# Attention and a sinkhorn-routed expert layer: raw first-layer weights on another queue and in another group, sums behind the adds in group 0, quarter products turned round in the fast pairs

## The chip, the cores and the metric

The kernel runs on one core of a Trainium2 chip. The time is device microseconds (us) of one execution. The engines of the core work side by side, each through its own instructions in order: TensorE (PE in the profile; PEld is its weight load), VectorE (DVE), ScalarE (ACT), GpSimd (POOL) and SyncE (SP). SP, ACT and POOL also issue DMAs. An engine that meets an instruction whose semaphore is not yet up stands still, and everything behind it on that engine stands with it.

## The reference

Inputs: local queries, keys and values of 8 batches x 8 heads x 512 x 64, and 32 global ones for each batch and head. Two steps:

```python
# attention: global rows see all; local row i sees the globals and local j with |i - j| <= 32
out_g = sm(scale * q_g @ k_all.T) @ v_all
out_l = sm(concat(scale * q_l @ k_g.T, masked(scale * q_l @ k_l.T))) @ concat(v_g, v_l)
x = rows of concat(out_g, out_l)             # 4352 tokens x 512
# expert layer: P is a 4352 x 8 matrix, normalised by rows and columns 8 times
P = sinkhorn(exp(x @ w_gate - max))
out = sum over e of P[:, e] * (relu(x @ w1[e]) @ w2[e])     # w1[e]: 512 x 1024, w2[e]: 1024 x 512
```

## The kernel before

Tokens are cut into nine groups: m = 0 to 7 of 512 local tokens, m = 8 with the 256 global ones. The first stage (to about 396 us) does the attention, the routing matrix and, in the gaps, the first layers of experts 0 to 3, whose hidden values go to DRAM (`hd`). The second stage, which the change touches, walks over *units* (m, e), with e in the order 4, 0, 5, 1, 6, 2, 7, 3. Unit i stands for m = i // 8. Units come in *pairs* of an even unit i (expert 4, 5, 6 or 7, whose first layer is still to be computed) and an odd unit i + 1 (expert 0 to 3, hidden values loaded by `load_h`). Pair 8 is units 8 and 9, the first of group 1; group 0 holds pairs 0, 2, 4, 6.

**The second layer** is a seven-product scheme: `product(i, q)`, q = 1 to 7, is 8 matmuls of 256 columns (2 token blocks x 4); q = 5, 2 and 1 take the sums `s` that `sums(i)` made on DVE, q = 6 and 7 the differences that `sums` wrote back into h, and q = 3 and 4 take h as it is. Products 1 to 5 add up in five fixed PSUM banks over the whole group; products 6 and 7 of a pair share two of three rotating banks (r0, r1, r2) and `add` (line 945, DVE) puts them into the output tile o in the odd unit. In the last unit of a group (`closes`) all banks are added to o, and `store` writes o out.

**The first layer of unit i + 2** is woven into the even body i: in the plain form `l1`, eight matmul groups of 4 x 512 columns, the first three of them before product 3; they use the same three rotating banks, so the second group needs the bank of product 6 and the third that of product 7 of the odd unit before.

**The fast form** (`class Fast`) takes two halves p = 0, 1 of 28 matmuls of 256 columns each, half 0 in body i - 2, half 1 in body i - 1, with stages s0 to s3: s0 (products 1 and 5 into banks H and Q, copied by ACT), s1 (2 and 6, and a DVE add X at line 862), s2 (7 and 3, and a DVE add Y at line 869), s3 (4 onto H). H sits in bank r0, whose last reader is the relu of s3 of the half before. It needs sums of first-layer weights. `WX` says from which group on an expert is fast. `prep_w1` makes the sums: a *raw piece* (half of an expert's w1, four strided DMAs of 128 KB, line 727) is loaded into a weight buffer, four DVE subtractions or additions (line 689) complete it, and POOL stores it to DRAM (`w1c`, line 742), from where it is loaded as a whole later (line 730). I call the four raw pieces R60, R61 (expert 6) and R70, R71 (expert 7).

**Queues.** `wseq` is the written order of all weight loads, plain ones (line 721, 1 MB), raw pieces and `w1c`. `load_w1` runs through it on SP, two ahead of use; all of them share the two buffers of the tag `w1e`. On SP they stand in one line with `load_pb` (row factors, line 753, 256 KB, two for a pair), `load_x` (line 770, once a group) and `load_h` (line 805, 1 MB). The order of all instructions is written by hand (`manual_schedule`). In an even plain body the DVE order is `sums(i + 1)`, `scale_x(i + 4)`, weight sums of the second layer in group 0 (`prep_w2c`, five instructions), `scale_h(i + 3)`, `prep_w1`; in an odd body `sums(i + 1)`, then the adds of products 6 and 7.

Of the kernel before, what the change touches and what calls it, by code (L numbers as in the profile page):

```python
# [23 lines left out]
def kernel(  # L24
# [13 lines left out]
    nc = tc.nc  # L38
# [3 lines left out]
    D, E = moe_w_gate.shape  # L42
# [30 lines left out]
    NL = E // 2  # L73
# [1 line left out]
    xd = [ydram.tile([P, DP, n], FP16, name=f"xd{m}") for m, (_, n) in enumerate(groups)]  # L75
    w1d = [ydram.tile([P, DP, F], FP16, name=f"w1d{e}") for e in range(NL, E)]
    pd = ydram.tile([E, NTOK], FP32, name="pd")
    WX = {6: 1, 7: 2}
    w1c = {e: [ydram.tile([P, 7, 2, 256], FP16, name=f"w1c{e}_{p}") for p in range(2)] for e in WX}
    psx = ExitStack()  # L80
    xpool = psx.enter_context(tc.tile_pool(name="xpool", bufs=1, side="right"))
# [623 lines left out]
    def fast(i):  # L705
        return i < NUN and units[i][0] < B and units[i][0] >= WX.get(units[i][1], B)

    wseq = [(i, p) for i in range(0, NUN, 2) for p in ((0, 1) if fast(i) else (None,))]
    for e, m in WX.items():
        for p in range(2):  # L710
            wseq.insert(wseq.index((E * m + 2 * p, None)), (e, "raw", p))
    raw = {}
    wnext = 0

    def load_w1(used):
        nonlocal wnext
        while wnext < len(wseq) and (wnext < 2 or wseq[wnext - 2] in used):
            i, *p = wseq[wnext]
            if p[0] is None:
                w = w1s[i] = wpool.tile([P, DP, F], FP16, tag="w1e", name="w1s")  # L720
                nc.sync.dma_start(out=w, in_=w1d[units[i][1] - NL])
            else:
                w = wpool.tile([P, 7, 2, 256], FP16, tag="w1e", name="w1q")
                if p[0] == "raw":
                    for o, r, k in ((0, 0, 0), (1, 0, 1), (3, 1, 0), (2, 1, 1)):
                        f0 = 512 * r + 256 * p[1]
                        nc.sync.dma_start(out=w[:, o], in_=w1d[i - NL][:, 2 * k : 2 * k + 2, f0 : f0 + 256])
                    raw[wseq[wnext]] = w
                else:
                    nc.sync.dma_start(out=w, in_=w1c[units[i][1]][p[0]])  # L730
                    w1s[(i, p[0])] = w
            wnext += 1
            if wnext < 2:
                return

    def prep_w1():
        for k in list(raw):
            w = raw.pop(k)
            for o, a, b, op in ((5, 0, 3, ALU.subtract), (3, 3, 2, ALU.add), (4, 3, 0, ALU.subtract),
                                (6, 1, 4, ALU.subtract)):  # L740
                tt(w[:, o], w[:, a], w[:, b], op)
            nc.gpsimd.dma_start(out=w1c[k[0]][k[2]], in_=w)
            used.add(k)
# [136 lines left out]
    def sums(i, k0=0, k1=HF, part=(0, 1)):  # L880
        if i >= NUN - 1:
            return
        n = groups[units[i][0]][1]
        t1, t2 = slice(0, n // 2), slice(n // 2, n)
        h = hs[i]
        if i not in ss:
            new_s(i)
        s = ss[i][:, :, k0:k1]
        lo, hi = h[:, k0:k1], h[:, HF + k0 : HF + k1]
        if 0 in part:  # L890
            tt(s[:, 0:2, :, 0 : n // 2], lo[:, :, 0:n].rearrange("p k (a t) -> p a k t", a=2),
               hi[:, :, 0:n].rearrange("p k (a t) -> p a k t", a=2), ALU.add)
            tt(s[:, 2, :, 0 : n // 2], lo[:, :, t1], hi[:, :, t2], ALU.add)
        if 1 in part:
            tt(lo[:, :, t2], lo[:, :, t2], lo[:, :, t1], ALU.subtract)
            tt(hi[:, :, t1], hi[:, :, t1], hi[:, :, t2], ALU.subtract)
# [12 lines left out]
    def closes(i):  # L909
        m, e = units[i]  # L910
        return e == (ORDER[-1] if m < B else ORDER[-2])

    def product(i, q):
        m, e = units[i]
        n = groups[m][1]
        nt = n // P // 2
        first = e == ORDER[0]
        h, s, w = hs[i], ss[i], w2c[e]
        lhs = {1: (s[:, 2], 0), 2: (s[:, 1], 0), 3: (h[:, 0:HF], 0), 4: (h[:, HF:FT], n // 2),
               5: (s[:, 0], 0), 6: (h[:, 0:HF], n // 2), 7: (h[:, HF:FT], 0)}[q]  # L920
        if q >= 6 and i % 2 == 0:
            pm = fixed[q] = ps_rot.tile([P, 512], FP32, tag=rot(), name="pm")
        elif first:
            pm = fixed[q] = ps_fix.tile([P, 512], FP32, tag=f"m{q}", name=f"m{q}")
        else:
            pm = fixed[q]
        for t in range(nt):
            for k in range(HF):
                nc.tensor.matmul(pm[:, HD * t : HD * (t + 1)], lhs[0][:, k, lhs[1] + P * t : lhs[1] + P * (t + 1)],  # L929
                                 w[:, k, q - 1, :], start=(k == 0 and t == 0 and (first if q < 6 else i % 2 == 0)),  # L930
                                 stop=(k == HF - 1 and (closes(i) if q < 6 else i % 2 == 1 or closes(i))),
                                 skip_group_check=True)
# [141 lines left out]
    for i, (m, e) in enumerate(units):  # L1074
        if i == NUN - 1:
            last_pair(i)
        elif i % 2 == 0:
            alloc_h(i + 2)
            load_pbs(i)
            if (i + 4) % E == 0:  # L1080
                load_x((i + 4) // E)
            load_h(i + 3)
            load_w1(used)
            if fast(i):
                sums_x(i + 2, (4,))
                sums(i, 2, 4)
            if fast(i + 2):
                f = Fast(i + 2, 0)
                if not fast(i):
                    sums(i + 1, part=(0,))  # L1090
                f.s0()
                product(i, 3)
                f.s1()
                product(i, 4)
                product(i, 5)
                sums(i + 1, part=(0,) if fast(i) else (1,))
                f.s2()
                used.add((i + 2, 0))
                if fast(i):
                    sums(i + 1, part=(1,))  # L1100
                scale_x(i + 4)
                if not fast(i):
                    scale_h(i + 3, 0, HF)
                product(i, 2)
                product(i, 1)
                f.s3()
                nrot = 0
                product(i, 6)
                product(i, 7)
                continue  # L1110
            if i + 2 < NUN:
                sums(i + 1)
            else:
                n = groups[m][1]
                h = hs[i + 1]
                s = ss[i + 1] = xsp.tile([P, HF, n], FP16, tag="xs", name="sl")
                tt(s, h[:, 0:HF, 0:n], h[:, HF:FT, 0:n], ALU.add)
            scale_x(i + 4)
            if m == 0:
                for e in {2: (2,), 4: (7,), 6: (3,)}.get(i, ()):  # L1120
                    prep_w2c(e)
            sums_x(i + 4)
            scale_h(i + 3)
            prep_w1()
            for fm in range(3):
                l1(i + 2, fm, ps_rot, rot())
            for q, fm in ((3, 3), (4, 4), (5, 5), (2, 6), (1, 7), (6, None), (7, None)):
                product(i, q)
                if fm is not None:
                    l1(i + 2, fm, ps_rot, rot())  # L1130
                if closes(i):
                    add(i, q, fixed[q])
            used.add((i + 2, None))
        else:
            if i >= E * B - 1:
                load_h(i + 4)
            load_w1(used)
            load_pbs(i)
            if fast(i + 1):
                f = Fast(i + 1, 1)  # L1140
                for q in (6, 7):
                    product(i, q)
                    add(i, q, fixed[q])
                late = fast(i - 1)
                scale_h(i + 2, *((0, HF) if late else (HF, FT)))
                product(i, 3)
                f.s0()
                product(i, 4)
                f.s1()
                sums_x(i + 3, (5,))  # L1150
                product(i, 5)
                product(i, 2)
                sums(i + 1, 0, 2, part=(0,))
                f.s2()
                sums(i + 1, 0, 2, part=(1,))
                if late:
                    scale_h(i + 2, HF, FT)
                sums_x(i + 3, (7, 6))
                product(i, 1)
                f.s3()  # L1160
                used.add((i + 1, 1))
                nrot = 0
                continue
            sums(i + 1)
            for q in (6, 7, 3, 4, 5, 2, 1):
                product(i, q)
                if q >= 6 or closes(i):
                    add(i, q, fixed[q])
            if closes(i):
                store(m)  # L1170
    ctx1.__exit__(None, None, None)
# [30 lines left out]
```

## Time and profile before

| what | value |
|---|---|
| median of 3 runs | 1058.3 us (1057.76 to 1060.25) |
| the profiled execution | 1056.72 us, its span 1055.0 us |
| PE busy | 1018.8 us (97%) |
| DVE busy | 873.7 us (83%) |
| second stage | about 396 us to the end; pairs 0 to 14 of groups 0 and 1 up to 563 us |

A pair of plain units takes 19.13 us of PE without a wait (464.04 to 483.17 us). A row of the timeline gives the start, the time from the first start to the last end, the engine, line and operation, output and inputs, the number of merged instructions, and in brackets how long the engine stood idle before it and what ended that.

### The profile page before, as it was taken

What the parts mean: (1) busy time and instruction counts of PE and PEld (TensorE: products, weight loads), DVE (VectorE), ACT (ScalarE), POOL (GpSimd) and SP (SyncE); (2) the same over time, 40 slices, a digit from 0 to 9 for tenths busy, and PEclk for the clock granted to TensorE, in tenths of its full rate; (3) what the DMA queues carried; (4) which work ended last, traced back from release to release, by engine and by line L of the source; (5) the groups of instructions that cost most, each with busy time, mean ns of one, the idle gap of its engine ahead of it and who ended that gap; (6) DMA issues with size and microseconds to landing.
All of it is one profiled execution on the core that took longest, in us unless ns stands there. A gap on an engine that the chain in (4) does not pass through costs nothing.

```text
span 1055.0 us, 22767 instructions
## 1 busy us (share of the span) xinstructions
PE 1018.8 (97%) x9166; PEld 732.2 (69%) x9166; DVE 873.7 (83%) x1651; ACT 514.4 (49%) x1300; POOL 139.5 (13%) x227
## 2 busy tenths in 40 slices
PE   7899999999999999998999999999999999999998
PEld 4555555555554466676877877877877878878887
DVE  8687777777775767979879889889899899898895
ACT  7777878787785674222323332333333332332331
POOL 7442332413413002000000000000000000000000
PEclk9899999999999999999999999999999999999999
DMA  9887688988946989845656636455553554464470
GB/s 262 189 216 210 124 265 201 205 235 187 226 130 169 290 277 300 227 156 219 198 183 255 200 145 218 158 186 184 191 190 139 201 185 167 168 210 155 142 262 23
DMA packets 102105, 206.88 MB, mean 196 GB/s; under 512 B 33952, under 2 KB 68208, under 8 KB 90864
## 3 DMA queue, kind: packets, MB, share of 16 engines
q1 hardware_dynamic: 56208, 163.54, 44.9%
q0 software_dynamic: 43184, 32.26, 17.6%
q10 hardware_dynamic: 2608, 9.64, 2.4%
q8 instruction: 72, 1.18, 0.5%
q14 instruction: 33, 0.27, 0.1%
HBM read 169.43 MB, written 57.29 MB: 215 GB/s over the span
## 4 chain that ended last, share of the span: by engine, by line
issue 47%; PE 27%; DVE 12%; ACT 8%; DMA 4%; SPq 1%; POOL 1%; ACTq 0%; DVEq 0%; POOLq 0%
PE ph L468 14%; ACT Pu L311 4%; DVE Pu L348 3%; DVE h L689 3%; PE m L929 3%; PE ph L819 2%; PE ptw L359 1%; ACT hT L471 1%; ACT qbd L285 1%; PE pm L929 1%; DMA w1c<-w1q 1%; DMA h<-hd 1%; DVE s L689 1%; DVE w2c L689 1%; PE pt L275 1%
## 5 line engine op out<-in xcount | busy, mean ns | idle before, releaser
L468 PE MATMUL ph<-xT,w1e 128*128 128x512 f16 (+1 forms) x1152 | 255.9, 367 | 0.2
L929 PEld LDWEIGHTS <-h 128*128 128x128 f16 x2160 | 211.8, 98 | 36.7 <-issue 0.8
L929 PE MATMUL m<-w2c,s 128*128 128x256 f16 x1620 | 199.9, 273 | 0.0
L821 ACT ACTIVATE h<-ph 128x512 f16<-128x512 f32 (+1 forms) x184 | 102.7, 560 | 192.9 <-PE ph L819 184.9
L929 PEld LDWEIGHTS <-s 128*128 128x128 f16 x1620 | 158.5, 98 | 29.8
L819 PE MATMUL ph<-xs,w1s 128*128 128x512 f16 (+1 forms) x736 | 169.5, 364 | 4.8 <-DVE o L945 4.7
L468 PEld LDWEIGHTS <-w1e 128*128 128x128 f16 x1152 | 105.4, 98 | 96.0 <-issue 3.0
L689 DVE TENSOR_TENSOR h<-h,pb 128x2048 f16<-128x2048 f16 (+1 forms) x49 | 152.5, 3112 | 4.7 <-DMA h<-hd 4.7
L689 DVE TENSOR_TENSOR s<-h 128x1024 f16<-128x1024 f16 (+2 forms) x168 | 126.5, 795 | 15.8 <-PE m L929 8.7
L929 PE MATMUL m<-w2c,h 128*128 128x256 f16 x1080 | 138.2, 274 | 0.0
L471 ACT ACTIVATE hT<-ph 128x512 f16<-128x512 f32 (+1 forms) x192 | 104.3, 558 | 47.6 <-PE ph L468 45.3
L929 PE MATMUL pm<-w2c,h 128*128 128x256 f16 x1080 | 123.8, 273 | 0.0
L819 PEld LDWEIGHTS <-w1s 128*128 128x128 f16 x736 | 72.5, 99 | 56.8 <-issue 7.7
L844 ACT ACTIVATE h<-pf 128x512 f16<-128x512 f32 x104 | 59.4, 596 | 97.2 <-PE pf L837 92.5
L689 DVE TENSOR_TENSOR xs<-xg,pb 128x2048 f16<-128x2048 f16 (+1 forms) x36 | 78.0, 2168 | 22.2 <-DMA pb<-pd 22.2
L311 ACT ACTIVATE Pu<-ms,mx 128x160 f16<-128x160 f32 x224 | 93.6, 420 | 5.7 <-DVE mx L308 3.3
L473 DVE TENSOR_SCALAR hT<-ph 128x512 f16<-128x512 f32 x96 | 66.1, 688 | 31.3 <-PE ph L468 30.6
L689 DVE TENSOR_TENSOR h<-h 128x1024 f16<-128x1024 f16 (+1 forms) x168 | 90.4, 580 | 0.0
L837 PEld LDWEIGHTS <-w1q 128*128 128x128 f16 x728 | 71.2, 98 | 13.4 <-issue 5.2
L308 DVE CUSTOM_DVE_ANT_0 ms<-sc,mask 128x160 f32<-128x160 f32 x224 | 59.9, 319 | 17.9 <-PE sc L303 17.4
L948 POOL DMA_DIRECT2D out_dram<-o x8 | 6.1, 757 | 461.6 <-DVE o L945 461.6
L837 PE MATMUL pf<-xs,w1q 128*128 128x256 f16 x416 | 58.1, 272 | 4.1 <-ACT h L844 4.1
(165 smaller groups left out, 1196.2 us busy)
## 6 DMA issues: line engine op xcount, KB each, us to landing
h<-hd SPq DMA_DIRECT2D x32, 1024.0 KB
hd<-hT SPq DMA_DIRECT2D x26, 1024.0 KB
w1s<-w1d SPq DMA_DIRECT2D x23, 1024.0 KB
w1q<-w1c SPq DMA_DIRECT2D x26, 896.0 KB
pb<-pd SPq DMA_DIRECT2D x64, 256.0 KB
w2c<-in_moe_w_dram POOLq DMA_DIRECT2D x16, 512.0 KB, 21.0
out_dram<-o POOLq DMA_DIRECT2D x8, 1024.0 KB, 4.6
f<-in_q_l_dram SPq DMA_DIRECT2D x15, 512.0 KB
```

What stands on the lines that cost most here:

```text
L308: nc.vector.tensor_tensor_reduce(out=ms[:, ii, :], in0=sc[:, SW * ii : SW * (ii + 1)], in1=mask[:, mi, :], scale=-scale, scalar=BIG, op0=A ...
L311: nc.scalar.activation(out=d["Pu"][:, i, :], in_=ms[:, ii, :], func=AF.Exp, scale=-1.0, bias=d["mx"][:, i : i + 1], accum_out=d["sm"][:, i ...
L348: nc.vector.tensor_tensor(out=d["Pu"][:, i0:i1, 0:KW], in0=d["Pu"][:, i0:i1, 0:KW], in1=d["rs"][:, i0:i1].unsqueeze(2).to_broadcast([P, i1 ...
L468: nc.tensor.matmul(ph[:, 0:n], wts[e][:, dk, P * fm : P * (fm + 1)], xT[m][:, dk, :], start=(dk == 0), stop=(dk == DP - 1))
L471: nc.scalar.activation(out=hT[:, fm, 0:n], in_=ph[:, 0:n], func=AF.Relu)
L473: nc.vector.tensor_scalar(out=hT[:, fm, 0:n], in0=ph[:, 0:n], scalar1=0.0, scalar2=None, op0=ALU.max)
L689: nc.vector.tensor_tensor(out=out, in0=in0, in1=in1, op=op)
L819: nc.tensor.matmul(ph[:, 0:n], w1s[i][:, dk, P * fm : P * (fm + 1)], xss[i][:, dk, 0:n], start=(dk == 0), stop=(dk == DP - 1))
L821: nc.scalar.activation(out=hs[i][:, fm, 0:n], in_=ph[:, 0:n], func=AF.Relu)
L837: nc.tensor.matmul(bank[:, 256 * c : 256 * (c + 1)], self.w[:, self.sta[q], k, P * c : P * (c + 1)], self.mov[q][:, k], start=(first and c ...
L844: nc.scalar.activation(out=self.h[:, k : k + 2, 256 * c : 256 * (c + 1)], in_=bank.rearrange("p (k t) -> p k t", k=2), func=AF.Relu)
L929: nc.tensor.matmul(pm[:, HD * t : HD * (t + 1)], lhs[0][:, k, lhs[1] + P * t : lhs[1] + P * (t + 1)], w[:, k, q - 1, :], start=(k == 0 and ...
```

## The change

1. `WX`: expert 6 is fast from group 2 on, not from group 1. Unit 12 (group 1, expert 6) gets the plain first layer.
2. `wseq`: the raw pieces stand before the loads of units 10, 12, 14 and 16 (before: R60 and R61 ahead of units 8 and 10, R70 and R71 ahead of 16 and 18). Their four DMAs each are issued by POOL, not SP.
3. `prep_w1` is skipped in group 0; the weight sums so fall into bodies 8, 10, 12 and 14.
4. In odd bodies of group 0, `sums(i + 1)` comes behind the adds of products 6 and 7.
5. In an even fast body whose next even unit is fast too (body 8 m + 4, m = 2 to 7, six times), product 3 comes ahead of s0, product 4 between s0 and s1, and products 5 and 2 ahead of s2, so that only product 1 stands between s2 and s3. Before: s0, 3, s1, 4, 5, s2, 2, 1, s3.

```diff
-    WX = {6: 1, 7: 2}
+    WX = {6: 2, 7: 2}
...
-    for e, m in WX.items():
-        for p in range(2):
-            wseq.insert(wseq.index((E * m + 2 * p, None)), (e, "raw", p))
+    for j, (e, p) in enumerate((e, p) for e in WX for p in range(2)):
+        wseq.insert(wseq.index((E + 2 * j + 2, None)), (e, "raw", p))
...
-                        nc.sync.dma_start(out=w[:, o], in_=w1d[i - NL][:, 2 * k : 2 * k + 2, f0 : f0 + 256])
+                        nc.gpsimd.dma_start(out=w[:, o], in_=w1d[i - NL][:, 2 * k : 2 * k + 2, f0 : f0 + 256])
...
-                f.s0()
-                product(i, 3)
-                f.s1()
-                product(i, 4)
-                product(i, 5)
-                sums(i + 1, part=(0,) if fast(i) else (1,))
+                if fast(i):
+                    product(i, 3)
+                    f.s0()
+                    product(i, 4)
+                    f.s1()
+                    product(i, 5)
+                    product(i, 2)
+                    sums(i + 1, part=(0,))
+                else:
+                    f.s0()
+                    product(i, 3)
+                    f.s1()
+                    product(i, 4)
+                    product(i, 5)
+                    sums(i + 1, part=(1,))
                 f.s2()
...
                 if not fast(i):
                     scale_h(i + 3, 0, HF)
-                product(i, 2)
+                    product(i, 2)
                 product(i, 1)
                 f.s3()
...
-            prep_w1()
+            if m > 0:
+                prep_w1()
...
-            sums(i + 1)
+            if m > 0:
+                sums(i + 1)
             for q in (6, 7, 3, 4, 5, 2, 1):
                 product(i, q)
                 if q >= 6 or closes(i):
                     add(i, q, fixed[q])
+                if q == 7 and m == 0:
+                    sums(i + 1)
```

## The prediction

> **What bounds the kernel now.** I read the page first: PE is busy 97% of the span, so only its idle time and its own work can pay. Then the waits, for what ends PE's idle time in the second stage, and the PE timeline for their places.
>
> ```profile
> PE 1018.8 (97%) x9166; PEld 732.2 (69%) x9166; DVE 873.7 (83%) x1651; ACT 514.4 (49%) x1300; POOL 139.5 (13%) x227
> ...
> PE ph L819 <- DVE o L945: 4.7, 2, 2.7
> ...
> PE pf L837 <- ACT h L844: 4.1, 6, 0.7
> ```
>
> Eight waits: two on the adds of products 6 and 7, six on a relu. In the timeline:
>
> ```profile
> 441.03 1.03 PE L819 MATMUL ph<-xs,w1s 128*128 128x512 f16 x4
> 444.09 2.35 PE L819 MATMUL ph<-xs,w1s 128*128 128x512 f16 x8 [2.04 <-DVE o L945]
> ...
> 483.17 1.03 PE L819 MATMUL ph<-xs,w1s 128*128 128x512 f16 x4
> 486.87 3.29 PE L819 MATMUL ph<-xs,w1s 128*128 128x512 f16 x8 [2.67 <-DVE o L945]
> ...
> 600.18 0.60 PE L837 MATMUL pf<-t,w1q 128*128 128x256 f16 x4
> 601.47 0.60 PE L837 MATMUL pf<-xs,w1q 128*128 128x256 f16 x4 [0.69 <-ACT h L844]
> ```
>
> Bodies 4 and 8 stop after their first l1 group. The cost is more than the idle time: the windows after it (columns: stretch, length, busy time of PE, PEld, DVE, ACT, POOL, then granted clock, DMA) show half the clock for 3.4 us.
>
> ```profile
> 445.37:448.79 3.42, 3.42 (x13) 1.82 (x12) 3.42 (x5) 0.98 (x2) 0.00 (x0) 0.50 0.64 271
> 464.04:483.17 19.13, 19.13 (x147) 14.09 (x144) 14.18 (x15) 5.97 (x10) 0.00 (x0) 1.00 0.50 166
> ```
>
> The DVE timeline says why: the adds (o<-pm) stand behind work that nobody awaits so soon.
>
> ```profile
> 481.47 1.80 DVE L689 TENSOR_TENSOR w1q<-w1q 128x512 f16<-128x512 f16 x4
> 483.19 1.82 DVE L689 TENSOR_TENSOR s<-h 128x2048 f16<-128x2048 f16 x2
> 484.92 1.29 DVE L689 TENSOR_TENSOR h<-h 128x1024 f16<-128x1024 f16 x2
> 486.13 1.28 DVE L945 SCALAR_TENSOR_TENSOR o<-pm,o 128x512 f32<-128x512 f32 x2
> 487.32 5.07 DVE L945 SCALAR_TENSOR_TENSOR o<-m,o 128x512 f32<-128x512 f32 x8
> ```
>
> **What goes.** Body 4: its first three l1 groups take 2.59 us unhindered; from 441.03 to 449.23 (where the clock is full again) 8.20 us passed for work of 4.34, so 3.86 go. In the new order DVE does the adds from 440.41, when scale_h ends; the first ends at 441.1, PE needs it at 441.03 + 0.87 = 441.9. Body 8: from 483.17 to 489.99 6.82 us for 2.59, 4.23 go; without weight sums (1.80) and with the sums of values (2.94) behind, the adds wait for nothing but product 7. The sums moved back hurt nobody: product 3 and 4 take h as it is, product 5 comes 6 us into the body. Six fast turns: four matmuls of 0.109 us from 600.18 hand over at 600.62, the next starts at 601.47: 0.85 each (0.69 idle by the row, the rest pipeline), 5.10 in six. Product 3 (8 x 0.109 = 0.87) now covers the relu. Between s2 and s3 one product of cover is lost: DVE has X (0.61 net), part 0 of the sums (1.74), Y (0.70) to do, 3.3 us with the hand-overs after s1; PE has products 5, 2 and 1 and the eight matmuls of s2, 32 x 0.109 = 3.49. Cover 0.18 left, before 1.06. Lower bound of this gain nothing, upper 5.10; I take 5.0, since DVE stood idle 1.06 us before X at 604.35.
>
> **What comes.** Unit 12 plain: 32 x 0.217 = 6.94 for 56 x 0.109 = 6.12, +0.82, and its fast work on DVE goes. The number of weight sums stays 16.
>
> The costly part is the weight buffers. In the built program R60 goes into the second buffer, unit 10 and then R61 into the first, and **unit 12's 1 MB load into the buffer of R60**: it waits for R60's store. Likewise 14 behind R61, 16 behind R70. Before, only pieces and w1c loads stood behind stores, far ahead of use. Now body 10 cannot begin before this chain is done: weight sums in body 8, store, load of 12. And that load stands on SP ahead of the row factors and hidden values that DVE needs before the next weight sums (body 10). So the chain paces three pairs:
>
> Pairs 4 and 6 at 19.13 put body 8 at 441.03 + 38.26 = 479.3. Products 6 and 7 of unit 7 end 4.2 us before (in the trace 475.31 + 32 x 0.109, and 0.17 of the last one's run, against 483.17), and DVE goes on without a break: second add 0.65, sums 2.94, eight closing adds 5.0, sums 2.94, scale_x 2.21, scale_h 4.34, weight sums 1.80: done at 475.1 + 19.9 = 495.0. POOL issues 0.29 later (458.84 to 459.13 before). What stands behind a store on SP goes out this much after its issue (timeline of POOL, then of SP):
>
> ```profile
> 459.13 0.55 POOL L742 DMA_DIRECT2D w1c<-w1q  x1 [49.88 <-DVE w1q L689]
> ...
> 464.03 1.91 SPq L727 DMA_DIRECT2D w1q<-w1d  x4
> ```
>
> 4.90 there, 3.86, 4.49 and 4.18 at the others, mean 4.36. So 12's load is issued at 499.7. By the landing records 1 MB with nothing ahead takes 4.71 to 4.91 (issues at 475.50 to 609.08), so body 10 starts at 504.6 instead of 498.4.
>
> Next round: behind a w1c load, two row factors and h landed h 10.80 after the first issue (487.42) and 10.06 (563.94); with 1 MB ahead 10.7. scale_x is done by then (8.1 + 2.2). Then 4.34 + 1.80 + 0.29 + 4.36: the load of 14 goes out 21.5 after that of 12, at 521.2, and body 12 starts at 526.1. Third round, with the 512 KB of load_x in the line (h landed 8.40 after the row factor before it at 440.52, with load_x between, and 7.67 and 7.62 without it at 504.10 and 579.80: 0.8, taken as 0.9): 22.4, load of 16 at 543.6, landed 548.5. Body 14 starts at **548.6** instead of 544.01, with all gains in group 0 already in it: **+4.6**. The half clock after the waits of bodies 10 and 12 is hidden in the chain; the one after body 14 (wait 548.6 - 526.2 - 19.13 = 3.3) costs the mean of the two seen (1.67 and 1.40): **+1.5**. The six turns: **-5.0**. Sum +1.1: 1056.72 + 1.1 = 1057.8 of the profiled execution, which stands 1.6 under the median, so **1059.4**. Behind body 14 I find no third effect: the w1c load of unit 20 also waits for a store (R71's), but is needed two pairs later.
>
> A rule of the Trainium skill (TensorE: Matmul & The Clock Gate, Part 1 on the clock gate) has the half clock follow only an idle window of about 3.4 us. The rows above disagree: 2.04 and 2.67 were enough. By the rule the wait of 3.3 would just escape it and the sum would be -0.4 instead of +1.1; the rows decide.
>
> POOL's new work: 16 issues instead of the SP's, at some 0.55 to 0.75 each by its own rows, on a queue that otherwise waits 461.6 us for adds. store(0) stands ahead of R60's store and is gone by 484; R61's issues wait for the l1 of unit 10 and R60's store, not the other way round. SP loses 1.9 us of issues a piece.
>
> **Bounds.** Three stores at 3.86 or 4.90 each: -1.5 or +1.6; h at 10.06 or 10.80: -0.7 or +0.4; half clock -0.1 or +0.2; turns 0 to +5.0. Without the last, which has its own rival, 1057.1 to 1061.6. No row shows a raw piece loaded by POOL. Its nearest rows are SP's: 2.1 us landing at 543.38, 5.4 at 525.07 next to other loads. Below nothing is excluded: R61, R70 and R71 go out with the store or beside the loads of the chain and add bytes there. At 5.4 - 2.1 = 3.3 for each of three rounds the end is +9.9. I take nothing, because in the first round the piece follows the store in its queue and is through before the load's bytes move.
>
> **The rivals.**
> 1. *The raw pieces on POOL delay the chain (slower).* Place: 512 KB between a store and the 1 MB load behind it. For: h lands 9.57 after the first row factor at 520.57, where a raw piece runs beside it, 7.6 without. Against: the 1 MB at 536.35 landed in 4.71 beside a store. It decides from 0.7 us a round (2.1 in all, to pass +3.2). At half of the 3.3: +5.0, 1064.4. A sentence of the Trainium skill belongs here (DMA: Bandwidth & Descriptors, SWDGE vs HWDGE vs iDMA): GpSimd writes the descriptors of its DMAs in SBUF and VectorE can lock it out. The four stores before took 0.53 to 0.55 to issue while DVE ran on, so no row bears a price out.
> 2. *The loads are not in the way (faster).* Weight sums done by 479.3 + 9.5 would leave no wait at body 10. They come 6.2 us too late by my sum; scale_h alone (4.34) would not be enough. Then 3.86 + 4.23 + 5.0 - 0.82 = 12.3 go: 1046.0.
> 3. *The quarter order gains nothing (slower).* Y comes later than s3 wants, because X or the sums start more than 0.18 late. With a new wait as long as the old: +6.1, 1064.4. Against: the same stages in the odd body have one product between s2 and s3 and no wait (599.31 to 600.18).
>
> **How the numbers follow.** A difference under 0.3% (3.2 us) is about what a measurement of this kernel can't tell from no change. My forecast, 1059.4 within its own 1057.1 to 1061.6 or a little off, has 0.52 (all but a little of it within 0.3%); rival 1 0.20, rival 3 0.10, rival 2 0.10, and 0.08 for a shorter chain than worked out (a third of it past -3.2). Faster 0.13, same 0.54, slower 0.33. The range reaches to 1065.5, over the prices of rivals 1 and 3, and to 1055.0 below, which a chain 4.4 shorter over its three rounds would give; rival 2 and the far end of rival 1 are left out.
>
> **What would show it.** Right: no PE wait at bodies 4 and 8, none before s0 at about 600; PE waits of about 6, 1 to 2 and 3 us at the starts of bodies 10, 12 and 14, ended by DMA w1s<-w1d; SP waiting for w1c<-w1q in front of those loads; body 14 near 548.6. Wrong: no such PE waits, or starts beyond 551, or a wait before s3 ended by DVE line 869 (after: 868).

## The result and the profile after

| | median | runs | ratio to before |
|---|---|---|---|
| before | 1057.25 us | 12 (1054.46 to 1060.25) | |
| changed | 1062.55 us | 12 (1060.24 to 1063.95) | 1.0049 [1.0036, 1.0062] |

The change makes the kernel slower by 5.3 us, where I had forecast +1.1. The profiled execution took 1063.95 us, its span is 1062.2. In this profile the second stage begins about 0.98 us later than in that of before; where I compare a time with the prediction, 0.98 is taken off. This execution was also the slowest of the twelve, so the two profiles lie further apart than the medians.

From the page, and from the waits:

```profile
PE 1022.0 (96%) x9142; PEld 730.8 (69%) x9142; DVE 869.1 (82%) x1638; ACT 512.7 (48%) x1296; POOL 151.2 (14%) x243
...
PE ph L818 <- DMA w1s<-w1d: 13.7, 2, 8.3
```

The two waits for the adds and the six for the relu are gone. In their place stand two long ones for 1 MB weight loads. Their places, in the PE timeline:

```profile
480.27 2.75 PE L818 MATMUL ph<-xs,w1s 128*128 128x512 f16 x12
...
507.85 4.71 PE L818 MATMUL ph<-xs,w1s 128*128 128x512 f16 x12 [8.28 <-DMA w1s<-w1d]
...
528.95 2.75 PE L818 MATMUL ph<-xs,w1s 128*128 128x512 f16 x12
...
553.64 5.30 PE L818 MATMUL ph<-xs,w1s 128*128 128x512 f16 x12 [5.40 <-DMA w1s<-w1d]
```

Body 8 starts at 480.27 and runs its three l1 groups through, where the kernel before stopped after the first. Bodies 10 and 14 wait for their weights, body 12 does not. Now the chain that ends in these loads: first DVE, then POOL, then SP.

```profile
494.11 1.80 DVE L689 TENSOR_TENSOR w1q<-w1q 128x512 f16<-128x512 f16 x4
```

```profile
496.21 0.55 POOL L741 DMA_DIRECT2D w1c<-w1q  x1 [10.43 <-DVE w1q L689]
496.80 2.82 POOL L726 DMA_DIRECT2D w1q<-w1d  x4
```

```profile
500.47 0.32 SPq L720 DMA_DIRECT2D w1s<-w1d  x1
...
522.10 0.32 SPq L720 DMA_DIRECT2D w1s<-w1d  x1
...
546.27 0.32 SPq L720 DMA_DIRECT2D w1s<-w1d  x1
```

Weight sums done at 495.91, store issued at 496.21, and directly behind it on POOL the four DMAs of R61, which waited for nothing but their turn in the queue. The load of unit 12 goes out at 500.47, that of 14 at 522.10, that of 16 at 546.27. The trace's landing records give the rest:

| load of unit | issued | the raw piece beside it on POOL, issued and landed | landed after | body starts |
|---|---|---|---|---|
| 12 | 500.47 | R61: 496.80 to 498.90, in by 502.45 | 7.33 | 507.85 |
| 14 | 522.10 | R70: 521.54 to 523.64, in by 530.36 | 5.69 | 528.95, no wait |
| 16 | 546.27 | R71: 542.69 to 544.79, in by 548.08 | 7.32 | 553.64 |
| 18 | 568.05 | none | 4.82 | |

The load of 12 comes in sixteen parts, and thirteen of them were in after 5.23 us; the last three came at 5.67, 5.99 and 7.33. Body 10 waits for the last one.

The clock after the two waits, as the windows show it (columns as before; the granted clock is the 0.50):

```profile
501.60:511.84 10.24, 3.99 (x10) 1.50 (x11) 3.41 (x4) 0.95 (x2) 0.00 (x0) 0.50 0.73 258
552.80:559.62 6.82, 5.98 (x17) 2.37 (x18) 3.85 (x2) 1.79 (x3) 0.00 (x0) 0.50 0.45 177
```

The second half clock begins at 552.80, 0.84 us before body 14, and body 14 runs at half the clock until 559.62.

**The balance.** Body 14 starts at 553.64 - 0.98 = 552.66 instead of 544.01: +8.65, with the gains of group 0 in it. From 553.64 to 560.05 PE did work of 3.47 us in 6.41: +2.94 for the half clock. The six turns: -5.1. Sum +6.5; the two spans differ by 7.2, less the 0.98 of the later start 6.2. This is the balance of the two profiled executions; the medians are 5.3 apart.

### The profile page after: what moved, and what is told of

Read it like the earlier page. It is cut to its first block, busy times and chain, and to the rows that moved or that the text cites. A ratio compares the mean times of both kernels' runs of the same rounds, so it can differ in the third digit from the quotient of the medians.

```text
span 1062.2 us, 22693 instructions
## 1 busy us (share of the span) xinstructions
PE 1022.0 (96%) x9142; PEld 730.8 (69%) x9142; DVE 869.1 (82%) x1638; ACT 512.7 (48%) x1296; POOL 151.2 (14%) x243
## 4 chain that ended last, share of the span: by engine, by line
PE 75%; ACT 7%; issue 7%; DVE 6%; DMA 4%; POOL 1%; SPq 0%; ACTq 0%; POOLq 0%; DVEq 0%
PE m L928 24%; PE ph L468 14%; PE ph L818 13%; PE pm L928 9%; PE pf L836 7%; ACT Pu L311 3%; DVE Pu L348 3%; DMA w1s<-w1d 1%; PE ptw L359 1%; ACT hT L471 1%; PE pv L157 1%; ACT qbd L285 1%; DMA w1c<-w1q 1%; PE pt L275 1%; DMA vraw<-in_v_l_dram 1%
## 5 line engine op out<-in xcount | busy, mean ns | idle before, releaser
L820 ACT ACTIVATE h<-ph 128x512 f16<-128x512 f32 (+1 forms) x192 | 107.4, 561 | 223.2 <-PE ph L818 218.4
L818 PE MATMUL ph<-xs,w1s 128*128 128x512 f16 (+1 forms) x768 | 179.1, 368 | 13.7 <-DMA w1s<-w1d 13.7
L818 PEld LDWEIGHTS <-w1s 128*128 128x128 f16 x768 | 76.0, 99 | 69.9 <-DMA w1s<-w1d 14.2
L689 DVE TENSOR_TENSOR xs<-xg,pb 128x2048 f16<-128x2048 f16 (+1 forms) x36 | 78.1, 2169 | 23.7 <-DMA pb<-pd 15.4
L843 ACT ACTIVATE h<-pf 128x512 f16<-128x512 f32 x96 | 55.0, 596 | 84.1 <-PE pf L836 80.0
L836 PEld LDWEIGHTS <-w1q 128*128 128x128 f16 x672 | 65.8, 98 | 7.6
L836 PE MATMUL pf<-xs,w1q 128*128 128x256 f16 x384 | 53.7, 273 | 0.0
```

The lines of the kernel that those rows point to most:

```text
L689: nc.vector.tensor_tensor(out=out, in0=in0, in1=in1, op=op)
L818: nc.tensor.matmul(ph[:, 0:n], w1s[i][:, dk, P * fm : P * (fm + 1)], xss[i][:, dk, 0:n], start=(dk == 0), stop=(dk == DP - 1))
L820: nc.scalar.activation(out=hs[i][:, fm, 0:n], in_=ph[:, 0:n], func=AF.Relu)
L836: nc.tensor.matmul(bank[:, 256 * c : 256 * (c + 1)], self.w[:, self.sta[q], k, P * c : P * (c + 1)], self.mov[q][:, k], start=(first and c ...
L843: nc.scalar.activation(out=self.h[:, k : k + 2, 256 * c : 256 * (c + 1)], in_=bank.rearrange("p (k t) -> p k t", k=2), func=AF.Relu)
```

## The experiments

My theory after the result: the chain through the two buffers is what costs, and the raw pieces on POOL make it 5 us longer than I had worked out. The rivals: the new places on POOL don't matter and the chain alone is longer; or the new quarter order does not pay. Later experiments ask which part of the change earns what, and what makes the loads late.

### 1. Weight buffers in turn

The edit also gives the two weights of the first stage that shared the tag `w1e` the new tags; that line is left out here.

```diff
...
-                w = w1s[i] = wpool.tile([P, DP, F], FP16, tag="w1e", name="w1s")
+                w = w1s[i] = wpool.tile([P, DP, F], FP16, tag=f"w1e{(wnext + (wnext > 12)) % 2}", bufs=1, name="w1s")
...
-                w = wpool.tile([P, 7, 2, 256], FP16, tag="w1e", name="w1q")
+                w = wpool.tile([P, 7, 2, 256], FP16, tag=f"w1e{(wnext + (wnext > 12)) % 2}", bufs=1, name="w1q")
```

R61 then goes into the buffer of R60 and unit 12 into that of unit 10: raw pieces wait for stores, and each 1 MB load only for the l1 groups of the plain unit before it.

> The changed kernel with one thing different: the two weight buffers are given out by position in the written order of loads, so that the four raw pieces follow each other in the second buffer and the plain loads of units 8 to 18 in the first. No load of a plain weight waits for a store of weight sums any more; the work, its order on every engine and the queues are the same. Theory (the chain store of weight sums, then 1 MB load, paces bodies 10, 12 and 14): PE waits at bodies 10 and 14 (8.28 and 5.40 us in the changed kernel) and the half clock behind them are gone, all that the change saves stays: the two stops of group 0 (3.9 and 4.2 us), six turns (5.1), less 0.8 for unit 12: about 12 us under the kernel before, ratio 0.988 to 0.990. Rival (the weight sums or the raw pieces themselves are too much for group 1, wherever they lie): waits of several us stay at bodies 10 to 14, ratio 1.000 or more.

Measured: 1043.68 us, ratio 0.9884 [0.9869, 0.9899]. In the second stage PE has no wait left but one of 0.6 us on an add near the end, which the kernels before and after have too. Its timeline, and POOL's:

```profile
497.49 2.75 PE L818 MATMUL ph<-xs,w1s 128*128 128x512 f16 x12
516.62 2.75 PE L818 MATMUL ph<-xs,w1s 128*128 128x512 f16 x12
535.76 2.75 PE L818 MATMUL ph<-xs,w1s 128*128 128x512 f16 x12
```

```profile
494.29 0.55 POOL L741 DMA_DIRECT2D w1c<-w1q  x1 [10.42 <-DVE w1q L689]
502.44 2.82 POOL L726 DMA_DIRECT2D w1q<-w1d  x4 [7.61 <-DMA w1c<-w1q]
```

The bodies follow each other every 19.13 us, and the wait for the store now stands on POOL (7.61 us), where nothing urgent is behind it. So with the pieces on POOL, all that the change lost goes when the pieces lie in the other buffer (run 7 has the same buffers with the pieces on SP). This version beats both kernels.

### 2. Raw pieces on SP

```diff
-                        nc.gpsimd.dma_start(out=w[:, o], in_=w1d[i - NL][:, 2 * k : 2 * k + 2, f0 : f0 + 256])
+                        nc.sync.dma_start(out=w[:, o], in_=w1d[i - NL][:, 2 * k : 2 * k + 2, f0 : f0 + 256])
```

> The changed kernel with the raw pieces issued by SP again, the buffers as in the changed kernel. There R61 and R71 go out from SP well before the store is done, so that they don't run into the 1 MB load. Theory (the chain paces the three pairs, and pieces from POOL just ahead of the 1 MB loads of units 12 and 16 make these 7.3 us long instead of 4.8): PE still waits at bodies 10 and 14, but the loads land in about 4.8 to 5; body 14 starts 3 to 4 us earlier than in the changed kernel, ratio to the kernel before about 1.001. Rival (the long loads have another cause, such as row factors and hidden values behind them in the same queue): loads stay at 7.3, ratio about 1.005.

Measured: 1057.16 us, ratio 1.001 [0.9997, 1.0023]. The PE timeline:

```profile
505.00 5.30 PE L818 MATMUL ph<-xs,w1s 128*128 128x512 f16 x12 [5.42 <-DMA w1s<-w1d]
...
527.70 2.76 PE L818 MATMUL ph<-xs,w1s 128*128 128x512 f16 x12 [0.72 <-DMA w1s<-w1d]
...
549.84 2.76 PE L818 MATMUL ph<-xs,w1s 128*128 128x512 f16 x12 [2.83 <-DMA w1s<-w1d]
```

SP issued R61 from 491.75 to 493.19, and the pieces were in by 495.50, 4.5 us ahead of the load of 12 (issued 500.05, landed after 4.90). The load of 16 took 4.79. The load of 14 went out right behind R70's pieces, which were in 1.7 us after it, and took 6.35: pieces on SP can make a load late as well. On the whole this is nearly the chain that the prediction worked out (+1.1). The 4.1 us between the two ratios (some 2 us either way, by the intervals) belong to the pieces on POOL. Between the two profiled executions it is 6.8 us, counted from body 4 on; 2.9 of these are the half clock behind body 14, which this run does not have.

### 3 and 4. The quarter order

Run 3 is the changed kernel with the old order (its edit is shown), run 4 the kernel before with the new one (the reverse edit).

```diff
-                if fast(i):
-                    product(i, 3)
-                    f.s0()
-                    product(i, 4)
-                    f.s1()
-                    product(i, 5)
-                    product(i, 2)
-                    sums(i + 1, part=(0,))
-                else:
...
+                f.s0()
+                product(i, 3)
+                f.s1()
+                product(i, 4)
+                product(i, 5)
+                sums(i + 1, part=(0,) if fast(i) else (1,))
...
```

> The changed kernel with the old order of the quarter products in the six fast bodies (s0, 3, s1, 4, 5, s2, 2, 1, s3). Theory: six waits of 0.69 us before s0 come back, 0.85 each with the pipeline, 5.1 us more than the changed kernel, ratio to the kernel before about 1.010. Rival (product 3 only moves the wait to another place): same as the changed kernel, 1.005.

> The kernel before with the new order of the quarter products alone. Theory: 5.1 us less, ratio 0.995; the two stops of group 0 stay. Rival (the turns' gain needs the rest of the change, or s3 waits for the DVE add at line 869 instead): ratio 0.998 to 1.000.

Measured: run 3 1066.43 us, ratio 1.0098 [1.0082, 1.0114]; run 4 1051.13 us, ratio 0.9952 [0.9936, 0.9967]. Taking the new order out of the change costs 0.49% (5.2 us), putting it into the kernel before saves 0.48% (5.1 us). The waits of run 3, then those of run 4:

```profile
PE pf L836 <- ACT h L843: 4.1, 6, 0.7
```

```profile
PE ph L819 <- DVE o L945: 5.3, 2, 3.3
```

In run 3 the six turns are back, in run 4 only the two stops of group 0 are left. The part stands on its own.

### 5 and 6. The sums behind the adds, without the rest

Run 5 is the kernel before with part 4 of the change alone, run 6 with parts 4 and 5. In both the weight sums of R61 stay in body 8, and unit 12 stays fast.

```diff
-            sums(i + 1)
+            if m > 0:
+                sums(i + 1)
             for q in (6, 7, 3, 4, 5, 2, 1):
                 product(i, q)
                 if q >= 6 or closes(i):
                     add(i, q, fixed[q])
+                if q == 7 and m == 0:
+                    sums(i + 1)
```

> The kernel before, with one part of the change: in group 0 the sums of hidden values go behind products 6 and 7 and their adds (the weight sums of body 8 and the third pair of expert 6 stay in group 0, the raw pieces stay on SP, the quarter order stays old). Theory (the two stops of group 0 came from the adds standing behind these sums, and the weight sums of body 8 need not move for them): both stops go, -3.9 and -4.2 us, and no load waits behind a store close to its use: 1049 us, ratio 0.992 to 0.993; no PE wait on an add in the second stage, the six turns of 0.85 us stay. Rival 1 (the weight sums had to go for body 8's stop to go): only the first stop goes, ratio 0.996. Rival 2 (sums that come later are late for product 5): a new PE wait on s in bodies 4 and 8, ratio 0.996 to 1.000.

> The kernel before, with the sums of group 0 behind the adds and the new quarter order, without the move of unit 12 to a plain unit and without the new places of raw pieces and weight sums. Theory: the gains add, -8.1 and -5.1: 1044 us, ratio 0.987 to 0.988, about that of the changed kernel with its buffers in turn (0.988); then the plain unit 12 and the moved raw pieces are worth nothing of their own, and the whole cost of the change lies in them. Rival (the move of the weight sums was needed): ratio 0.991 to 0.992, so that the move has a value of some 4 us which its chain of loads then loses.

Measured: run 5 1053.86 us, ratio 0.9984 [0.997, 0.9998]; run 6 1049.21 us, ratio 0.9944 [0.9929, 0.9959]. The theory was wrong in both. In run 6 the rival holds: the move of the weight sums was needed. In run 5, rival 1 has the mechanism (only the first stop goes) but not the size: part 4 alone is worth 1.7 us (interval 0.2 to 3.2), not 8. No wait on `s` came, so rival 2 falls, though the ratio lies in its range. Run 5's PE timeline in body 8, and DVE's:

```profile
479.88 1.03 PE L819 MATMUL ph<-xs,w1s 128*128 128x512 f16 x4
482.23 1.89 PE L819 MATMUL ph<-xs,w1s 128*128 128x512 f16 x8 [1.32 <-DVE o L945]
486.37 1.87 PE L929 MATMUL m<-w2c,h 128*128 128x256 f16 x8 [2.25 <-DVE o L945]
```

```profile
479.78 1.80 DVE L689 TENSOR_TENSOR w1q<-w1q 128x512 f16<-128x512 f16 x4
481.49 1.28 DVE L945 SCALAR_TENSOR_TENSOR o<-pm,o 128x512 f32<-128x512 f32 x2
482.69 1.82 DVE L689 TENSOR_TENSOR s<-h 128x2048 f16<-128x2048 f16 x2
484.42 1.29 DVE L689 TENSOR_TENSOR h<-h 128x1024 f16<-128x1024 f16 x2
485.63 5.07 DVE L945 SCALAR_TENSOR_TENSOR o<-m,o 128x512 f32<-128x512 f32 x8
```

The stop of body 4 is gone. In body 8 the weight sums (1.80) still hold the first adds, so the l1 groups stop (1.32); and the sums of values, now behind those adds, hold the eight adds that close group 0, so product 3 stops too (2.25), because its bank is among them. From 479.88 to 490.64 PE did work of 5.22 in 10.76 us and lost 5.54, where the kernel before lost 4.23; 0.77 more goes in a wait on `w2c` just ahead. Together -3.9 + 1.3 + 0.8 = -1.8; measured -1.7.

In run 6 the same stops, 1.32 and 2.25, cost 3.88 (9.10 us for 5.22), since no half clock follows. Run 6 gains 5.9 us, run 1 gains 12.3. So by the ratios, moving the weight sums out of body 8 (part 3, and with it the plain unit 12) is worth about 6 us, some 2 either way. Between the two profiled executions, from body 4 to the end, it is 3.4, which fits what run 6 still loses (3.9 in the stops and 0.3 in a wait on `w2c`) less the 0.8 that the plain unit 12 costs. Whichever size holds, the move belongs to the change as much as the sums behind the adds do.

### 7. Buffers in turn and raw pieces on SP

The edits of runs 1 and 2 together.

> The changed kernel with the weight buffers in turn, as in the version at 0.988, but with the raw pieces issued by SP. Theory (with buffers in turn, a raw piece waits for a store of the weight sums; on POOL it waits in a queue where nothing urgent stands behind it, on SP the row factors, hidden values and 1 MB loads stand behind it): PE waits of 3 to 7 us come back at bodies 10, 12 and 14, ratio 1.000 to 1.007. Rival (the turn of the buffers alone removes the chain, whatever queue has the pieces): ratio 0.987 to 0.990 and no PE wait in the second stage.

Measured: 1063.0 us, ratio 1.0083 [1.0063, 1.0102]. SP's timeline, then PE's:

```profile
497.74 1.91 SPq L726 DMA_DIRECT2D w1q<-w1d  x4
499.75 0.41 SPq L720 DMA_DIRECT2D w1s<-w1d  x1
```

```profile
504.69 4.37 PE L818 MATMUL ph<-xs,w1s 128*128 128x512 f16 x12 [7.42 <-DMA w1s<-w1d]
```

The load of 12 waits for no store here, but stands on SP behind a piece that does: it goes out at 499.75, where in run 1 (pieces on POOL) it went out at 489.82. Bodies 12 and 14 wait too (3.03 and 2.12). So the queue of the pieces, harmful with the change's buffers, is what lets the buffers in turn work: the two have to be chosen together.

This run also has loads right behind pieces that SP issued. The pieces were in 1.7, 1.7 and 2.0 us after the loads of 12, 14 and 16 went out, as late as POOL's in the changed kernel (2.0 for 12, 1.8 for 16), and by the packet records their bytes moved as long beside the load (to 1.4 to 1.7 us after its issue here, to 1.4 to 1.6 there). Yet the loads of 12 and 16 took 4.90 and 5.00, where the changed kernel took 7.33 and 7.32; that of 14 took 6.88. So pieces still on their way do not make a load late every time, and POOL is not needed for it.

### 8. Raw pieces on ACT

```diff
-                        nc.gpsimd.dma_start(out=w[:, o], in_=w1d[i - NL][:, 2 * k : 2 * k + 2, f0 : f0 + 256])
+                        nc.scalar.dma_start(out=w[:, o], in_=w1d[i - NL][:, 2 * k : 2 * k + 2, f0 : f0 + 256])
```

> The changed kernel with the raw pieces issued by ACT instead of POOL, buffers as in the change. Theory A (the late last parts of the 1 MB loads of units 12 and 16 come from the pieces' bytes moving beside them, whatever queue they come from): those loads land again after 6 to 7.5 us where the pieces go out within 4 us before them, ratio 1.003 to 1.007. Theory B (they come from POOL's queue, whose packets are served otherwise): the loads land within 5.2 us even with the pieces beside them, PE waits as with the pieces on SP (5.4, 0.7, 2.8), ratio 0.999 to 1.002. ACT may be held at a piece that waits for its buffer; then a PE wait on ACT h or relu stands in the waits and the ratio says nothing of either.

Measured: 1056.26 us, ratio 1.0006 [0.9989, 1.0022], with the waits

```profile
504.13 4.39 PE L818 MATMUL ph<-xs,w1s 128*128 128x512 f16 x12 [5.43 <-DMA w1s<-w1d]
...
525.27 2.76 PE L818 MATMUL ph<-xs,w1s 128*128 128x512 f16 x12 [0.20 <-DMA w1s<-w1d]
...
548.25 4.45 PE L818 MATMUL ph<-xs,w1s 128*128 128x512 f16 x12 [3.67 <-DMA w1s<-w1d]
```

at bodies 10, 12 and 14. These are the numbers of theory B, but not for its reason: on ACT the pieces stand behind no store, so R61 went out at 490.94 to 492.39 and R71 at 536.89 to 538.34 and were in 4.4 and 2.2 us ahead of the loads of 12 and 16, which took 4.91 and 4.83. Only R70 ran beside a load (that of 14, 5.39; its last piece was in 5.0 us after the load went out). Place and queue are not told apart by this run; the next three do that.

### 9. The store behind the next pieces

The buffers of the change, the pieces on POOL, but `prep_w1` only notes the store, and `store_w1` issues it behind the next raw piece (or, where none comes, ahead of the next load). The lines left out keep each tile in the buffer that it has in the change.

```diff
...
                     raw[wseq[wnext]] = w
+                    store_w1()
...
-            nc.gpsimd.dma_start(out=w1c[k[0]][k[2]], in_=w)
+            owed.append((k, w))
...
```

> The changed kernel with the same buffers, the raw pieces still on POOL, but each store of weight sums put behind the next raw pieces in POOL's queue instead of ahead of them. Theory (the pieces went out beside the 1 MB loads only because they stood behind the store in POOL's queue): R61's pieces go out near 491 and are in before the load of 12 goes out near 499.5; the loads of 12 and 16 land in under 5.3 us instead of 7.3; PE waits about as with the pieces on ACT (5.4, 0.2 to 0.8, 3 to 3.7); ratio 0.999 to 1.002. Rival (pieces on POOL's queue disturb whatever their place, or their store is now late behind them): ratio 1.004 to 1.007 and a wait of 8 us at body 10 again.

Measured: 1065.7 us, ratio 1.0101 [1.0079, 1.0122], above both forecasts. Both sides had a part of it. PE, then POOL:

```profile
503.02 5.30 PE L831 MATMUL ph<-xs,w1s 128*128 128x512 f16 x12 [5.32 <-DMA w1s<-w1d]
529.65 4.05 PE L831 MATMUL ph<-xs,w1s 128*128 128x512 f16 x12 [4.68 <-DMA w1s<-w1d]
554.72 5.16 PE L831 MATMUL ph<-xs,w1s 128*128 128x512 f16 x12 [4.47 <-DMA w1s<-w1d]
```

```profile
490.13 2.83 POOL L737 DMA_DIRECT2D w1q<-w1d  x4 [6.22 <-PE ph L831]
494.34 0.56 POOL L721 DMA_DIRECT2D w1c<-w1q  x1 [1.38 <-DVE w1q L689]
517.41 2.82 POOL L737 DMA_DIRECT2D w1q<-w1d  x4 [22.51 <-PE ph L831]
520.23 0.56 POOL L721 DMA_DIRECT2D w1c<-w1q  x1
```

With the pieces in before the load, all three loads land in 4.79, 4.83 and 4.83 us, although POOL issued the pieces. But in the second round the weight sums were done at 514.0, and the store stood until 520.23 behind R70's pieces, which wait for the l1 groups of body 10 and then take 2.8 us to issue; so body 12 waits 4.68. Either order on POOL's one queue costs: pieces behind the store run into the load, pieces ahead of it hold the store.

### 10 and 11. The loads by themselves

One trial of run 11: `mark` is a small VectorE write that lets the DMAs behind it go; `wc` is the 896 KB store, `pieces` the four raw pieces on the queue under test, and the last line the 1 MB load, which must wait for the store. Two row factors and another 1 MB follow on SP. Run 10 has neither the store nor the row factors. Each of the two runs is a single execution. In all trials of run 11 but those with POOL's pieces, the lines left out put one addition of VectorE (0.7 us) between the store and the marks of the pieces.

```python
mark(w[:, 0, 0:1])
nc.gpsimd.dma_start(out=wc, in_=wq)
...
for o in range(4):
    mark(r[:, o, 0, 0:1])
pieces()
...
nc.sync.dma_start(out=w, in_=wd[0])
```

> Only the loads, none of the reference's work (the output is zeros): eight times each, a 1 MB load on SP with a second 1 MB behind it, about 3.6 us after the first of four raw pieces of 128 KB goes out, the pieces on no queue, on SP, on ACT, on POOL with VectorE at work, and on POOL with VectorE idle. Theory A (bytes): alone 4.8 us as in the profile before, and with pieces 5.3 to 7.5 on every queue alike. Theory B (queue): on SP and ACT within 0.5 us of alone, on POOL 1.5 us or more above alone. If VectorE's work delays POOL's pieces, the two POOL cases differ in the pieces' own landing by 0.5 us or more.

> Again only loads and stores, none of the reference's work (the output is zeros), now with the traffic of body 8 of the changed kernel: a 896 KB store on POOL, a 1 MB load on SP that waits for it, two row factors and another 1 MB behind it; beside it no pieces, or the four raw pieces issued 0.6 to 2.8 us after the store by POOL, by SP or by ACT; and, without the store, the pieces issued 1.6 to 2.4 us ahead of the load by each of the three queues. Twelve trials each. Theory A (bytes that are still moving make parts of the 1 MB load late, on every queue): with the store, the load takes 4.8 us without pieces and 6 to 7.5 us with pieces by POOL, SP and ACT alike. Theory B (POOL's queue): 6 to 7.5 us with POOL's pieces, under 5.3 us with SP's and ACT's. Theory C (neither: what else moved in the changed kernel): under 5.3 us in all.

In run 10 the pieces began 4.5 us ahead of the load, not 3.6 (an addition of VectorE took 0.69 us), and landed early: those of SP and ACT 0.6 to 0.9 us before the load went out, those of POOL by 0.5 to 0.8 us after it (one trial: 1.7). The 1 MB took 4.7 to 4.8 us with and without pieces, on every queue, so the queue alone, at that distance, costs nothing. VectorE's work did not matter either: POOL took 722 ns an issue with VectorE at work and 721 with it idle, and the pieces landed after 2.7 and 2.6 us.

Run 11 has the traffic of the changed kernel (rows: issues, KB of each, median us to landing):

```profile
w_none<-wd SPq DMA_DIRECT2D x12, 1024.0 KB, 4.8
...
w_pool<-wd SPq DMA_DIRECT2D x12, 1024.0 KB, 6.9
...
w_sp<-wd SPq DMA_DIRECT2D x12, 1024.0 KB, 5.1
...
w_act<-wd SPq DMA_DIRECT2D x12, 1024.0 KB, 5.0
...
w_npool<-wd SPq DMA_DIRECT2D x12, 1024.0 KB, 5.8
...
w_nsp<-wd SPq DMA_DIRECT2D x12, 1024.0 KB, 5.4
...
w_nact<-wd SPq DMA_DIRECT2D x12, 1024.0 KB, 5.5
```

With pieces by POOL behind the store the load takes 6.9 (5.2 to 8.0), with pieces by SP or ACT 5.1 and 5.0, without pieces 4.8. That is theory B, with two reserves. Behind the store POOL's last piece landed 1.7 to 2.5 us after the load went out (one trial: 3.6), those of SP and ACT 1.4 to 1.6 after it (one trial: 2.5, with a load of 5.49): the pieces of SP and ACT went out up to 0.8 us sooner. Without the store (`w_n...`), POOL's last piece went out 0.8 us after the load and those of SP and ACT 0.1 to 0.6 ahead of it, and the three lie closer together; beside SP's pieces two of these loads took 6.37 and 7.28, beside ACT's one took 6.82. So pieces still on their way make a load late often but not always, and with POOL's pieces behind a store it happens most. The 1.8 us may come from POOL's way of serving the pieces (the traces of the change and of run 7 have them in packets of 4096 bytes from POOL, of 512 from SP), from the store ahead of them in the queue, or from their landing up to 1 us later. No run here separates these; the two short loads of run 7 speak against the landing time alone.

## Why the prediction was right or wrong

- **The forecast as a whole.** The likeliest outcome, no change within 0.3%, did not come; the change is slower by 0.49%. The sum's own range, 1057.1 to 1061.6, is missed by about 1 us. The wide range holds 1062.55 only because it was drawn over the prices of rivals 1 and 3, and rival 1, given 0.20, is what happened. Of the signs of being wrong, one was met: body 14 starts at 552.66, beyond 551. Of the three waits named, two came, longer than forecast (8.28 for 6, 5.40 for 3), and that of body 12 did not.
- **Group 0, right.** Bodies 4 and 8 run through. Runs 1 and 6 show that this needed both the sums behind the adds and the weight sums out of body 8, as the sum for body 8 had it.
- **Six turns, right.** 5.0 predicted; runs 3 and 4 give 5.2 and 5.1. Rival 3 falls.
- **The chain through the buffers, right.** Load of 12 predicted to go out at 499.7, went at 499.5 (less the 0.98); load of 14 predicted at 521.2, went at 521.1. Run 1 takes the chain away and gives the 12.3 us of rival 2's sum (1057.25 x 0.0116; the interval is 10.7 to 13.8, so that the tenth is chance; from body 4 to the end the two profiles differ by 12.2). As a rival it was false: the loads are in the way.
- **The raw pieces on POOL, wrong.** The step is "I take nothing, because in the first round the piece follows the store in its queue and is through before the load's bytes move". It follows the store, and just for that reason is in only 2.0 us after the load went out; by the packet records its bytes moved until 1.6 us after, those of the load from 1.1 on. Loads of 12 and 16 took 7.33 and 7.32 instead of 4.9, +2.4 each; the first has no sequel: body 12 waits for nothing, since h behind that load came only 0.6 late (11.26 us for 10.7) and SP went on 3.91 us after the next store's issue instead of 4.36. In the third round the pieces of R70 also ran beside the line of the load of 14, the row factors, `load_x` and h: h was in 13.49 us after the load of 14 went out, where I had 11.6, so the load of 16 went out 1.7 late (545.3 for 543.6). Most of this is not POOL's: the loads of 14 and 16 went out 24.2 us apart here, 23.7 with the pieces on SP (run 2) and 23.5 on ACT (run 8), where I had 22.4. The bound on h (-0.7 or +0.4) was too narrow in any case, and it doesn't follow from its own rows: 10.06 and 10.80 against 10.7, twice, give -1.3 and +0.2. 1.7 and 2.4 make the 4.1 by which body 14 misses 548.6 (552.66). Rival 1 had this mechanism and place, and a price of +5.0 for it; run 2 gives 4.1 back. Why pieces just there make parts of a load late stays open (run 11). The bounds had +9.9 as the far end, so the value was to be had; choosing zero against a row of 3.3 was the error.
- **Half clock after body 14, mis-sized.** 1.5 predicted, 2.94 measured: two windows at half the clock instead of one; the wait was 5.40 and not 3.3, and reached 0.84 us into the first of them. In run 2, with a wait of 2.83, there was none. So this term hung on the one above.
- **POOL's issues, right in size.** 0.70 us each (2.82 for four), and they delay nothing by their own time in the changed kernel.

The forecast of "within 0.3%" thus failed on one term, the raw pieces beside the loads, and on the half clock that hangs on it: +6.5 by the balance of the profiled executions, +5.3 by the medians, instead of +1.1.

## What to carry to other kernels

When tiles of one tag take turns in two buffers, look up in the built program which buffer each tile was given; what a load waits for is decided there, and with the pieces on POOL one other choice turned +0.5% into -1.2% (with the pieces on SP the same choice gave +0.8%). A DMA that must wait for a store belongs on a queue where nothing urgent stands behind it, and a DMA that needn't wait should not be queued behind a store when a load on the critical path follows that store; turning the two round is no cure where the DMA itself waits for something late (run 9). A gain that two edits give together (sums behind the adds, weight sums elsewhere) may be nearly absent when one is made alone.

## What the runs showed of the hardware

**One late part decides.** In run 11, in trials with POOL's pieces behind the store, twelve of the sixteen parts of the 1 MB were in by 5.8 us at the latest, and the last one to four came at up to 8.0. The Trainium skill (DMA: Bandwidth & Descriptors, Latency and other measured facts) says that two of the sixteen DMA engines are usually slower and guesses at the rings in which GpSimd's descriptors lie. The runs agree in that a few parts are late, and latest by POOL's queue; which engines they are, no record here shows. Without the store and with SP's pieces, where GpSimd issued nothing, one load also took 7.28 us, with three parts late, so GpSimd's descriptors cannot be the whole reason. The same page (SWDGE vs HWDGE vs iDMA) has VectorE lock GpSimd out of the memory that the descriptors go through while VectorE is in a 2-port mode. Run 10's additions on VectorE show no such price (722 against 721 ns an issue); whether they run in that mode, no run here shows.

**The clock looks at fixed windows.** The starts of half clock in a trace lie whole multiples of 3.413 us apart (before: 445.37 and 486.33, twelve of them). Idle time of 2.04 (before, body 4), 2.12 (run 7) and 2.25 us (run 5) within one such window brought the half clock for the next; 1.68 (run 6), 1.84 (run 4, body 4, a stop of 1.99) and again 1.84 (run 2, a wait of 2.83 cut in two) did not. The closest pair is 1.94 (run 8, from 497.23), which did not, and 2.01 (run 3, from 545.83), which did. So runs 5 and 6, with the same two stops, differ by the half clock. The windows of both:

```profile
479.88:490.64 10.76, 7.19 (x34) 3.71 (x32) 10.55 (x19) 2.39 (x4) 0.54 (x1) 0.84 0.53 187
```

```profile
480.29:489.39 9.10, 5.52 (x35) 3.11 (x33) 8.89 (x16) 2.39 (x4) 0.54 (x1) 1.00 0.48 180
```

The granted clock is 0.84 in the one and 1.00 in the other. A half window with 0.84 us idle was followed by another (the change, from 552.80), one with 0.76 was not (run 9, from 528.89). The Trainium skill (TensorE: Matmul & The Clock Gate, Part 1) has the free-running window of 3413 ns, which the trace bears out, and an idle window as what brings the half clock; here some 57 to 59% of a window was enough (1.94 not, 2.01 yes, of 3.41).
